# Attention, soft mixture of experts and a cosine-gated layer on one core: another written-out order of the attention's steps, with 86 instead of 91 of the exponentials' sums on VectorE

## The chip, the core and the metric

One core of a Trainium2 chip runs the whole program. The metric is the device time of one execution in microseconds (us), the median over repeated runs. The engines work side by side and meet through semaphores: TensorE (PE, with its weight loads shown as PEld), VectorE (DVE), ScalarE (ACT), GpSimd (POOL) and SyncE (SP), which issues most of the transfers (DMAs). Each engine takes its own instructions strictly in the order in which the program holds them, so an instruction that waits holds up all that stand behind it on that engine.

## What is computed

Three layers, cut to what matters here:

```
q_pool = q.reshape(B, H, S // 2, 2, D).mean(axis=3)          # B=4, H=8, S=1152, D=64
scores = matmul(q_pool, k.transpose) / sqrt(D)
attn   = exp(scores - max);  attn /= sum(attn) + 1e-9
x      = matmul(attn, v)                                     # to (2304, 512)
x      = soft_moe(x, phi, w1, w2)                            # 8 experts of 4 slots, F = 1024
h      = x @ w_in;  out = (h * cos(h)) @ w_out               # d_ff = 2048
```

The change touches the attention alone (with the first part of the mixture of experts and the preparation of later weights, which are woven into it).

## The kernel before, in words

The 32 heads are taken as 16 pairs (p = 0 to 15). Both heads of a pair stand side by side in the 128 partitions. A pair's 576 pooled queries are taken in two halves (a = 0, 1) of 288, and the 1152 keys in nine blocks (t = 0 to 8). What is done for a pair, with the names of the functions that record it and the lines of the profile:

- `load_q`, `load_k`, `load_v`: SP loads 576 KB each. `sum_q` (DVE, L347), `tr_q` and `tr_k` (PE transposes, L358, L382), `q_hi`, `k_hi` (ACT) and `q_lo`, `k_lo` (DVE, L369, L401) make the split operands.
- `max_pair` (PE, L415) makes scores of 128 queries with 384 keys for both heads, and `max_pair_red` (DVE, L424) reduces them to a maximum; 15 such for a pair. `max_neg` (DVE, L430), `max_row` (PE, L442) and `max_put` (ACT, L449) turn the negated maxima into a row that is added to the scores by a matmul.
- `scores` (PE, L460 and L463, eight matmuls), `exps` (ACT, L471), `av` (PE, L498, four instructions in the trace) and `av_out` for each half: the first run of five blocks goes out on ACT (L511), the second run of four is added on DVE (L513).
- `e_sum` (L486 for t = 1, L488 after it; L482 for one of the last pair) adds the exponentials of the nine blocks into a tile ES, one after the other: eight sums a half, each of which reads what the last one wrote. They run on DVE or on POOL; the table `VEC` says which.
- The denominators: `sum4` (PE, L523) sums ES over the partitions, `sum4_copy` (ACT, L530) copies it, `sum4_turn` (L535, a small transfer that ACT issues) spreads it over the partitions as `rt`, `sum4_rec` (DVE, L563) takes the reciprocal, `sum4_hi` (ACT, L567) and `sum4_lo` (POOL, L571) split it, `sum4_back` (L576, two small transfers) brings it back, `sum4_spread` (PE, L584) spreads it, and `pair_mul` (DVE, L589) multiplies the pair's result.
- Woven between: 32 weight conversions (`conv_load`, `conv_act` L289, `conv_low` L294 on ACT; `conv_clamp` L298, `conv_shift` L304, `conv_sign` L310 on DVE; `conv_round` L316 on POOL; `conv_store`), loads of the experts' weights (`ring_piece`, `late_piece`, L251), and for three of the four batches the statistics of the mixture (`b_...`).
- At the end: `run_min`, `run_turn`, `run_row`, `run_col`, `run_put` (L743 to L761) carry a running minimum over, and `fin_sum0`, `rec_mul` (L545 to L596), `l_xt`, `lt_mm`, `lt_max`, `lt_exp`, `l_x` finish the last pair's first half.

Nothing of this order comes from a scheduler at run time. All 2500 steps are made as a list, and `ORDER`, a string of two characters a step, says in which order they are recorded; each engine then gets its share in that order. Two things follow the order too: the four double banks of PSUM ("2") and the five tiles of exponentials ("E") are handed out by it, so the order also decides whose reader a step on TensorE has to wait for.

```
    for i in order:
        o = ops[i]
        assert all(d.done for d in o.deps)
        if o.take:
            o.spot = spots[o.take].pop(0)
        o.fn(o)
...
    def on_vector(p, a, t):
        return (p, a, t) == (NP - 1, 1, 1) or str(t) in VEC[2 * p + a]
```

After the attention (from some 489 us on) come the rest of the last pair, the experts (L1229, L1262) and the cosine layer (L1397 to L1443), whose code is not touched.

Of the kernel before, what the change touches and what calls it, by code (L numbers as in the profile page):

```python
# [52 lines left out]
)  # L53
ORDER = (
    "020304050709060G080H0A0OXsXt0PXu0Q0R0M0N0E0F0C0D0S0I0J0K0L2429010T2A0U0X0Y0V0b0W0m23250B2C0n0p0t0x0qXvXwXxXyXz26"
    "0u0-0y0c100h0i0o0s0w2D0Z0a0d2E0r0+12132F0e27X+2814150v0z2B1118191C1D160f0g1G1H2W0j2XX-Y1Y21A17Y01B1F1J0k0l2M1K2N"
    "2G1L1O1M1P1S1W1a2H1E1I2I1T2UY31X1Q1U474A1N1R1V1Z1b2V1d1e2J2O2PY41f1g2S2T1j1k1n1o2Q2R1Y1r1s2K1i2L1c482Y4D4E4H4I1h"
    "1l2b2c4JY64G1m1q4BY5Y74C2Z2a1u1v1p4F6C2j2k2q2r2t2u2l2m2x2y2-2h306B2i1t1wY81x334WY94K1y4X002s2w2+32YAYB4L3436372v"
    "2z2f2g2d383C393G3KYC2e2n3D31353H1z4f3A4S3B3E3L2obs6E2p3F3J1+YE1-YD4g3N3P3O4T4OYF3Q3S3W3a3I4P3T3XYHYI3b4Q4RYJ3e3U"
    "3Y4Y4Z4a3R3V3Z3dYG8Z3f3hYK203i3c4bYM4U4V3j3k3n3o3M4M3r3s3v4N4c6F3w3g6G6J4d3m3l3q3uYL3yYNYPYO4h49YQ4e3p3t3z4i4u4v"  # L60
    "4j4k4x4-534y4z503x544l4m57213+58226H6L3-YRYUbt514n4w4+6I6K6M6N52565A5B40YSYT4o55595C4p5D5G5K4q5O4r5H6O6a5L5P8c5E"
    "8a5F4s4tAd5J5N5R6b6UYVYW6P5I5M5SYX6V5T5W5U5XYY5a5b5e6S5YYZ5i5f416W6c6T6X5VYa6d5Z425d5hYb5j5lYc43446Y5m5c5g5kbu5n"
    "5r6Z5o5p5s6Q6R5v5Q5w6e6f5z5+6g6D6lbv6m8f8g8iYdYf8d6h6i8eYe5q5u5t5x5y60616y5-8q8h6z8r6-737071776pYgYhYi747B787C6q"
    "45468b6263648j8kAg6jYk8l6+72767A7E7F6k756n6o7G8m7H7K7L7O8n7S7P797D7T6r6s6tYjYl7J6u7N7R6v7V6wbwChbx7I6x8oAe8+7M65"
    "7W7Q667X7a8p7Y7e7i7b8-YnYoYp7m907f7c7j67997Z7d687g7n7k7oYs919AYm7h7l7p7q8w8x7r7sby8y8z7v7z7w817+8s8t8uYqYr7u8v7y"
    "8082AhAi9293947t7x7-83Al84857U9798YtYv9K9L9N9O9PAf696AYu9R9VYw9S9W9B9C9Z9aYxY+8687Aj88An95969M9QAk9TAmAo9UAp9Y9c"
    "9d9X9F9G9e9f9D9E9HYy9i9m9j9b9n898A9q9rCkA+A-8B8CYzAsAt9h9l9I9JY-Z09p9t9g9k9o9vZ1Z29u9w9yAu9zA09sA4A1bzAvA5A8Z3Z6"
    "A9B2B3AwAx9x9-9+8D8EZ4Ayb+AzZ5b-A3A7ABAC8J8KB0B18NA28OA6AAADAEAHAIAqArElALAPAMAQ8P8QB4B5B68FClAFZ78GAJAN8IB7CmCp"
    "Z9ZAB8AGAKAOASZ88H8T8LAT8UBBZBZCBO8MBCCiBPBJBKBRBSBVZDBZBWBaBDBE8VAR8WAUAV8RZE8SB9BABdBeBHAWBTBic0c1BICnBFBXBGCo"
    "ZFZGCqZHZIZJBQBUBLBYBcBjBbBfBgBhCrBmBqBuZKCsCtBkBnZMBrCuC+CvBlc2C-BpBtBvZLBxByBMD6AXBoBsBwEoCyBNAYAZD78X8YBzCzB+"  # L70
    "C0C4C1D4C5D5C8C2C9CCCHCDC6CAD0CwCxEmZNB-C3C7CID1CBCFCGD8ZOD9CLCMD2CPCQCTD3EpDADBCECJCNHAAaZPZQCKCOCSZRZSDCCUCjCR"
    "CVEqEtCWCXDSc3DTc4DDDVDEHDDWDXDZDaDdDFZTDeDhAbCYDGDiErZUAcDHCZCaDbDfc5DjEnEvDUDIDYDcEwExDgDJEsZVEuDKDmDnDLDMc6Dk"
    "Dlc7DNZWDOCbZXDoDqDrDPDuJEDyDvDzCcZYCdZZZaE+E-F4F5CeDpDsDtDxD-DQDRE0F0F1F2E1E2E4F3E5DwD+E6E8ECE9EDEyEzZcEGEHELF6"
# [1455 lines left out]
```

## Time and profile before

| | us |
|---|---|
| median of 3 runs (773.06 to 776.13) | 773.59 |
| the profiled execution, its own time | 778.18 |
| span of the profile (first to last instruction) | 776.4 |
| TensorE busy, of the span | 737.1 (95%) |
| VectorE busy | 587.7 (76%) |
| ScalarE busy | 448.9 (58%) |
| GpSimd busy | 409.5 (53%) |

The profiled execution took 4.59 us more than the median. All durations below are from it. Its span leaves 1.8 us of its time outside. A row of a group of instructions gives their number, the busy time, the mean duration of one, and the idle time of the engine before them with what ended it. The granted clock of TensorE stands as PEclk: 1.00 is 2.4 GHz, 0.50 is 1.2 GHz.

### The profile page before, as it was taken

The page shows a single profiled execution, that of the slowest core. Times are in us where ns is not written, and L with a number is a line of the kernel's source. Part 1 is how long each engine was busy: PE and PEld are TensorE (multiplying, and loading weights), DVE is VectorE, ACT ScalarE, POOL GpSimd, SP SyncE. Part 2 cuts the span into 40 slices and gives each one's busy share as a digit, 9 for nine tenths or more (in the row PEclk, how much of TensorE's full clock was granted, in tenths as well). Part 3 has the DMA queues.
Part 4 walks back from the last instruction along what each step waited for, and adds up shares of the span by engine and source line. Part 5 has one row for each costly group of instructions (what it writes and reads, how often), then busy time and mean ns, then how long its engine had stood idle before and what let it go on. Part 6 is the DMA issues. An engine that isn't in the chain of part 4 may idle for free.

```text
span 776.4 us, 16372 instructions
## 1 busy us (share of the span) xinstructions
PE 737.1 (95%) x6336; PEld 532.1 (69%) x6336; DVE 587.7 (76%) x935; ACT 448.9 (58%) x838; POOL 409.5 (53%) x340
## 2 busy tenths in 40 slices
...
GB/s 201 111 122 142 116 194 143 100 164 174 198 144 137 199 137 140 185 138 162 52 157 103 140 164 211 190 365 385 302 1 28 27 29 28 10 17 28 29 28 27
DMA packets 86482, 101.48 MB, mean 131 GB/s; under 512 B 48260, under 2 KB 48260, under 8 KB 86404
## 3 DMA queue, kind: packets, MB, share of 16 engines
...
q10 hardware_dynamic: 6020, 0.34, 0.6%
...
## 4 chain that ended last, share of the span: by engine, by line
PE 48%; DVE 9%; ACT 2%; issue 2%; POOL 1%; ACTq 0%; DVEq 0%; POOLq 0%
PE o L1433 16%; PE o L1435 8%; PE mx L498 6%; PE mx L460 4%; DVE nm L424 2%; PE po L1262 2%; PE u L1397 2%; PE h L1229 2%; PE mx L415 2%; DVE ES L488 1%; PE mx L463 1%; PE pm L1341 1%; POOL ES L488 1%; ACT E L471 1%; PE mx L442 0%
## 5 line engine op out<-in xcount | busy, mean ns | idle before, releaser
L488 POOL TENSOR_TENSOR ES<-ES,E 128x576 f32<-128x576 f32 x142 | 208.2, 1467 | 94.5 <-DVE ES L488 66.6
L424 DVE TENSOR_REDUCE nm<-mx 128x2 f32<-128x768 f32 x240 | 221.3, 950 | 26.7 <-PE mx L415 25.8
L471 ACT ACTIVATE E<-mx 128x576 f32<-128x576 f32 x288 | 177.4, 651 | 83.3 <-PE mx L463 62.6
L460 PE MATMUL mx<-Q,kX 64*128 64x288 f32 x1152 | 171.5, 314 | 9.9 <-DVE nm L424 4.7
L498 PE MATMUL mx<-E,vn 128*64 128x288 f32 x1152 | 157.7, 414 | 3.0 <-DVE nm L424 2.2
L1417 POOL TENSOR_TENSOR lo<-g,hi 128x512 fp32r<-128x512 f32 (+1 forms) x73 | 94.3, 1291 | 110.4 <-DVE hi L1415 106.1
L460 PEld LDWEIGHTS mx<-Q,kX 64*128 64x128 f32 x1152 | 111.8, 190 | 30.3 <-DVE nm L424 11.5
L498 PEld LDWEIGHTS mx<-E,vn 128*64 128x64 f32 x1152 | 75.8, 137 | 59.1 <-ACT E L471 8.0
L1433 PE MATMUL o<-w_hi,hi 128*128 128x512 f32 x288 | 113.1, 393 | 0.7 <-DVE hi L1415 0.7
L1435 PE MATMUL o<-w_lo,hi 128*128 128x512 f32 x288 | 113.2, 393 | 0.3 <-DVE w_lo L1321 0.3
L415 PE MATMUL mx<-kX,Q 64*128 64x384 f32 x480 | 87.6, 387 | 5.7 <-DVE nm L424 4.7
L460 PE MATMUL mx<-Q,kY 64*128 64x288 f32 x576 | 87.2, 297 | 0.0
L463 PE MATMUL mx<-NM,one_row 64*128 64x288 f32 x576 | 86.9, 296 | 0.0
L1433 PE MATMUL o<-w_hi,lo 128*128 128x512 f32 x288 | 77.4, 389 | 0.0
L1404 DVE SCALAR_TENSOR_TENSOR r<-t,u 128x512 f32<-128x512 f32 (+1 forms) x73 | 49.4, 679 | 36.4 <-ACT t L1402 35.8
L1402 ACT ACTIVATE t<-u 128x512 f32<-128x512 f32 (+1 forms) x73 | 43.0, 591 | 58.0 <-PE u L1397 57.9
L1413 DVE SCALAR_TENSOR_TENSOR g<-r,u 128x512 f32<-128x512 f32 (+1 forms) x73 | 49.6, 679 | 35.5 <-ACT r L1411 34.8
L316 POOL TENSOR_TENSOR cvt<-cvt 128x512 uint32<-128x512 uint32 x32 | 43.4, 1357 | 61.9 <-DVE cvt L310 28.7
L415 PEld LDWEIGHTS mx<-kX,Q 64*128 64x128 f32 x480 | 44.9, 190 | 28.6 <-DVE nm L424 10.9
L488 DVE TENSOR_TENSOR ES<-ES,E 128x576 f32<-128x576 f32 x81 | 61.5, 759 | 2.8 <-POOL ES L488 0.5
L1433 PEld LDWEIGHTS o<-w_hi,lo 128*128 128x128 f32 x288 | 54.1, 188 | 11.5
L1433 PEld LDWEIGHTS o<-w_hi,hi 128*128 128x128 f32 x288 | 54.2, 188 | 10.8 <-DVE hi L1415 0.9
...
## 6 DMA issues: line engine op xcount, KB each, us to landing
...
```

What stands on the lines that cost most here:

```text
L415: nc.tensor.matmul(out=m[:, h, 0:384], lhsT=Q1[p % 2][hs, AT[i]:AT[i] + 128], rhs=X[p][hs, ks], start=True, stop=True)
L424: nc.vector.tensor_reduce(out=nm3[p][:, i, :, c:c + 1], in_=m[:, :, 0:384], axis=AX.X, op=ALU.max)
L460: nc.tensor.matmul(out=sc[:, h, 0:HF], lhsT=x[hs, ks], rhs=y[hs, qs], start=(n == 0), stop=False)
L463: nc.tensor.matmul(out=sc[:, h, 0:HF], lhsT=one_row[hs, :], rhs=NM[p % 2][hs, qs], start=False, stop=True)
L471: nc.scalar.activation(out=e, in_=sc[:, :, 0:HF], func=AF.Exp, scale=1.0 / 16.0)
L488: eng.tensor_tensor(out=ES[p, a], in0=ES[p, a], in1=E[p, a, t], op=ALU.add)
L498: nc.tensor.matmul(out=av_t[p, a, g][64 * h:64 * h + 64, 0:HF], lhsT=vn[p][:, h, t, :], rhs=E[p, a, t][:, h, :], start=(t == g), stop=(t = ...
L1404: nc.vector.scalar_tensor_tensor(out=r, in0=t, scalar=MAGIC, in1=u, op0=ALU.subtract, op1=ALU.subtract)
L1413: nc.vector.scalar_tensor_tensor(out=g, in0=r, scalar=1.0, in1=u, op0=ALU.subtract, op1=ALU.mult)
L1417: nc.gpsimd.tensor_tensor(out=lo[:, 0:n], in0=g, in1=hi[:, 0:n].bitcast(FP32), op=ALU.subtract)
L1433: nc.tensor.matmul(out=o, lhsT=x, rhs=w_hi[ff], start=(ff == 0 and not part), stop=bool(part and ff == NF - 1))
L1435: nc.tensor.matmul(out=o, lhsT=x, rhs=w_lo[ff], start=False, stop=False)
```

## The change

`ORDER` is another string of the same 2500 steps, and `VEC` names other blocks for VectorE. No function is changed. Of the tables:

```
 VEC = (
-    "468", "1", "45", "2468", "25", "237", "4", "1267",
+    "58", "12", "6", "125", "1267", "1", "25", "1458",
...
-    "234", "17", "238", "137", "67", "123568", "2345678", "1234567",
+    "28", "168", "48", "", "1678", "368", "2345678", "1234567",
 )
 ORDER = (
-    "020304050709060G080H0A0OXsXt0PXu0Q0R0M0N0E0F0C0D0S0I0J0K0L2429010T2A0U0X0Y0V0b0W0m23250B2C0n0p0t0x0qXvXwXxXyXz26"
...
+    "Xs0203040705090A0S0B0T0O0P06240E0Q0I0R010GXt0J0F0K0L0H0C0M0N292D232E2A0D0U0V080W0m0pXuXv2F0nXw0q0r2C0t0u0x0h260y"
...
 )
```

Of the 256 sums 91 were on VectorE and 165 on GpSimd; now 86 are on VectorE and 170 on GpSimd. In the new order fewer steps on VectorE stand right behind the step that wrote what they read. Counted over the whole attention, such neighbours are: `conv_clamp` and `conv_shift` 20 before and 9 now, `conv_shift` and `conv_sign` 22 and 11, two sums on the same ES 25 and 13, `max_pair_red` and its `max_neg` 28 and 24, `b_stat` and `b_lg` 1 and 2.

VectorE around the reciprocal of pair 5 (`sum4_rec`, L563), before: the conversion's three steps and the maximum's negation (L430) are neighbours.

```order
L424 TENSOR_REDUCE nm_2664<-mx 128x2 x3
L563 RECIPROCAL rt<-rt 128x9
L298 TENSOR_SCALAR cvt<-cvt 128x512
L430 TENSOR_REDUCE Z<-nm_2664 128x4
L304 TENSOR_SCALAR cvt<-cvt 128x512
L310 SCALAR_TENSOR_TENSOR cvt<-raw,cvt 128x512
L424 TENSOR_REDUCE nm_3102<-mx 128x2 x2
```

The same place of the change:

```order
L430 TENSOR_REDUCE Z<-nm_2637 128x4
L298 TENSOR_SCALAR cvt<-cvt 128x512
L424 TENSOR_REDUCE nm_3058<-mx 128x2
L304 TENSOR_SCALAR cvt<-cvt 128x512
L488 TENSOR_TENSOR ES<-ES,E 128x576
L310 SCALAR_TENSOR_TENSOR cvt<-raw,cvt 128x512
L513 TENSOR_TENSOR avs<-mx,avs 128x288
L424 TENSOR_REDUCE nm_3058<-mx 128x2
L563 RECIPROCAL rt<-rt 128x9
L424 TENSOR_REDUCE nm_3058<-mx 128x2 x7
```

What moved: between the conversion's steps now stand steps that don't read them, and the reciprocal stands behind the conversion instead of ahead of it. Counted from the step that issues the transfer of `rt` (`sum4_turn`), VectorE has 13 steps ahead of this reciprocal, where it had 6. For other pairs it is the other way round: for pair 2 it has 3 where it had 9, for pair 6 it has 5 where it had 8.

VectorE in the last pair, before: four sums in a row (blocks 5 to 8 of the first half) stand ahead of the running minimum's copy (L761) and of pair 14's product (L589).

```order
L751 TENSOR_REDUCE mr<-mx 1x32
L513 TENSOR_TENSOR avs<-mx,avs 128x288
L488 TENSOR_TENSOR ES<-ES,E 128x576 x4
L761 COPY nM_118<-mx 32x1
L589 TENSOR_TENSOR xT<-avs,mx 128x576
L482 SCALAR_TENSOR_TENSOR ES<-E 128x576
L488 TENSOR_TENSOR ES<-ES,E 128x576 x2
L556 TENSOR_SCALAR rec<-mx 128x96
```

The same place of the change:

```order
L751 TENSOR_REDUCE mr<-mx 1x32
L488 TENSOR_TENSOR ES<-ES,E 128x576 x5
L513 TENSOR_TENSOR avs<-mx,avs 128x288
L589 TENSOR_TENSOR xT<-avs,mx 128x576
L488 TENSOR_TENSOR ES<-ES,E 128x576 x2
L482 SCALAR_TENSOR_TENSOR ES<-E 128x576
L761 COPY nM_118<-mx 32x1
L488 TENSOR_TENSOR ES<-ES,E 128x576 x2
L556 TENSOR_SCALAR rec<-mx 128x96
```

What moved: the product (L589) has come ahead of the last two sums of the first half. The copy (L761) has gone behind them, and so has, on TensorE, the small matmul that it reads (L758), which in the change stands behind the scores of blocks 1 to 4 of the second half instead of ahead of them. TensorE there before:

```order
L498 MATMUL mx<-E,vn 64x288 x8
L758 MATMUL mx<-ones,mr 32x1
L460 MATMUL mx<-Q_1_104,kX 128x288 x2
L460 MATMUL mx<-Q_1_104,kY 128x288 x2
L460 MATMUL mx<-Q_1_106,kX 128x288 x2
L463 MATMUL mx<-NM_108,one_row 128x288 x2
L584 MATMUL mx<-rh,pick 128x288 x2
```

And in the change:

```order
L463 MATMUL mx<-NM_108,one_row 128x288 x2
L758 MATMUL mx<-ones,mr 32x1
L498 MATMUL mx<-E,vn 64x288 x4
L545 MATMUL mx<-ES,ones 64x288 x2
L498 MATMUL mx<-E,vn 64x288 x6
L460 MATMUL mx<-Q_1_104,kX 128x288 x2
```

What moved: the sums over the partitions for the last pair's first half (L545) now follow the first two blocks of its second half, ahead of blocks 5 to 8; the matmul of the running minimum (L758) stands next to them.

## Rows read from the trace of the kernel before

**Rows 1.** Busy us (x instructions) of PE, PEld, DVE, ACT, POOL by stretch, clock, DMA share, GB/s.

```profile
20.00:480.00 460.00, 441.04 (x4750) 316.20 (x4752) 410.86 (x599) 282.79 (x524) 287.41 (x211) 0.99 0.51 145
...
210.40:213.70 3.30, 3.30 (x28) 3.30 (x30) 3.26 (x5) 1.30 (x2) 1.50 (x2) 0.50 0.91 279
473.20:476.50 3.30, 3.30 (x30) 3.02 (x28) 1.62 (x3) 1.07 (x3) 0.00 (x0) 0.50 0.72 253
500.00:520.00 20.00, 19.34 (x164) 6.83 (x158) 4.51 (x25) 4.55 (x12) 3.49 (x8) 1.00 1.00 345
```

**Rows 2.** Chain that ended last, 297 to 489 us: its shares by line.

```profile
by line: PE mx L498 23.7%; PE mx L460 15.8%; DVE nm L424 9.9%; PE mx L415 7.1%; DVE ES L488 5.5%; PE mx L463 4.7%; issue 4.4%; POOL ES L488 2.2%; ACT E L471 2.2%; PE mx L442 1.9%; DVE cvt L304 1.5%; DVE cvt L310 1.4%; DVE avs L513 1.4%; PE 
```

**Rows 3.** Waits of VectorE, 20 to 489 us: us in total, times, longest.

```profile
DVE nm L424 <- PE mx L415: 25.8, 47, 1.6
...
DVE rt L563 <- DMA rt<-rec: 2.6, 1, 2.6
```

**Rows 4.** Waits of TensorE, 20 to 489 us.

```profile
PE mx L460 <- DVE nm L424: 4.7, 8, 1.3
```

**Rows 5.** Groups by line: busy us, mean ns | idle before.

```profile
L488 POOL TENSOR_TENSOR ES<-ES,E 128x576 f32<-128x576 f32 x142 | 208.2, 1467 | 94.5 <-DVE ES L488 66.6
...
L488 DVE TENSOR_TENSOR ES<-ES,E 128x576 f32<-128x576 f32 x81 | 61.5, 759 | 2.8 <-POOL ES L488 0.5
```

**Rows 6.** VectorE by time, 455 to 458 us: start, us, what.

```profile
455.31 0.75 DVE L488 TENSOR_TENSOR ES<-ES,E 128x576 f32<-128x576 f32 x1
455.97 0.45 DVE L513 TENSOR_TENSOR avs<-mx,avs 128x288 f32<-128x288 f32 x1
...
457.00 0.42 DVE L298 TENSOR_SCALAR cvt<-cvt 128x512 f32<-128x512 f32 x1
457.34 0.15 DVE L743 TENSOR_TENSOR mrow<-nmst 128x1 f32<-128x1 f32 x1
```

**Rows 7.** The same from 34 us on.

```profile
34.17 0.42 DVE L298 TENSOR_SCALAR cvt<-cvt 128x512 f32<-128x512 f32 x1
34.62 0.43 DVE L304 TENSOR_SCALAR cvt<-cvt 128x512 uint32<-128x512 uint32 x1
```

**Rows 8.** The chain, 466 to 490 us: start, us, what.

```profile
470.29 0.77 DVE ES L488
...
471.16 0.76 DVE ES L488
```

**Rows 9.** VectorE, 466 to 479 us; in brackets the idle time before.

```profile
468.20 0.46 DVE L513 TENSOR_TENSOR avs<-mx,avs 128x288 f32<-128x288 f32 x1 [1.22 <-PE mx L498]
468.58 3.33 DVE L488 TENSOR_TENSOR ES<-ES,E 128x576 f32<-128x576 f32 x4
...
478.11 0.26 DVE L556 TENSOR_SCALAR rec<-mx 128x96 f32<-128x96 f32 x1 [2.94 <-PE mx L545]
```

**Rows 10.** TensorE, 472 to 475 us.

```profile
472.02 0.40 PE L460 MATMUL mx<-Q,kX 64*128 64x288 f32 x2 [2.26 <-DVE nM L761]
...
472.80 0.29 PE L460 MATMUL mx<-Q,kY 64*128 64x288 f32 x2
472.93 0.30 PE L460 MATMUL mx<-Q,kX 64*128 64x288 f32 x2
...
474.39 0.45 PE L460 MATMUL mx<-Q,kY 64*128 64x288 f32 x2
474.63 0.45 PE L460 MATMUL mx<-Q,kX 64*128 64x288 f32 x2
```

**Rows 11.** VectorE, 206 us.

```profile
206.75 0.21 DVE L563 RECIPROCAL rt<-rt 128x9 f32<-128x9 f32 x1 [2.58 <-DMA rt<-rec]
```

**Rows 12.** TensorE, 209 to 211 us.

```profile
209.42 0.44 PE L415 MATMUL mx<-kX,Q 64*128 64x384 f32 x2 [1.53 <-DVE nm L424]
210.29 0.65 PE L415 MATMUL mx<-kX,Q 64*128 64x384 f32 x2 [0.42 <-DVE nm L424]
```

**Rows 13.** ScalarE's queue, 198 us.

```profile
198.34 0.59 ACTq L535 DMA_DIRECT2D rt<-rec  x1
```

More of the change, by code (lines that the diff above doesn't have):

```diff
@@ L59 @@
[L59 to L63, printed above, removed]
@@ new lines @@
+    "3236372e2l2m38393C311z3D353A2n3G3HYD4O2o2p4P3K6E4f3PYFYH3E3Q3L3BYI1+3F3J4g3N3O4W1-204Y4X3S3T3W3a8Z3e3I4Z3X3U3b3M"
+    "3fYJ3Y4a4b4UYG4V3R3V3Z3d3h3i4MYK4N3j3n3k3o21223r3v6C3c3g3s4p4Q3l4R3pYM3w3t3xbs4c3m3q3uYL3y4q3z4nYN4l4d4e4o4m6F6G"
+    "6J4u4x4-494v4y5350YPYQ4z6H57YR544jYO4w584+5256YS5A51554k6I6K5B594h6L6M4i5C5D5E5G6N4r3+5H3-4s4t6c8c6S6dYU6T405K5L"
+    "5OYTYV5IYXYY5F5P5J5N5R5Tbt6n5M5QYW5S5U5W6o5X5a5e5i8a5bYZ5f6Y5Y5j5c414243445V5Z5g6Z6O6P6U6VYc6Qbu5d5h5l5n5k6D5m6R"
+    "5o6e6f5r5sYa5vYb6l5w6m5z5+6W6X8f8g6abv5q5u6bAd8d5p5t5x6g8i8e8h6h5y6i6061Yd45468j8k8l6y6-73Yf6z5-70Yg7177746j787B"
@@ new lines @@
+    "6k7C62Yh63758q6p6q8m8n6+72Ye8r64Yk767AYiYj7E7F6r797D6sbw7G7H8y7K8z7O7S7L7PYl7I657TYm6t8u6u6vYn7J7N7R7V6w8v6x7W90"
+    "918s7X7a7Y7M8t7b7Q7U7e7ibx667fYoYp7j8+Ae7m7r7v8-7c7nYq67688o8p7Z7gAg7d7h7sYs7l7p7q7w8wYr8x7z927+7k7o818295AhAiYt"
+    "Yu7t7x937u7y94Alby968084859B9C9K9LYv9N9O9R9V7-839S9P9W97989Z9a696A86Yw9T8788YxAjAnAk999AAo8bAp9M9Q9U9Y9cAmAy9dAz"
+    "Yy9e9f9i9m9j9X9b9gbz9Db+899nCh9E9q9rY+8AYz8B9F9h9G8C9H9l9p9I9JCkY-Z09tAf9k9u9vAu9y9wAvZ19o9zA09+A1A+A2A4A8A-A5As"
+    "Z2B2B3Z3b-c0A69x9-A3A7A9ABACZ4AtAwAxZ6ADAE8D8EAHAIZ5ALAMAqAAAFArAPAQB0B18F8GB4B58I8HBDAGAK9sCiB6Z7Z9ClZ8B7B8AOAS"
@@ new lines @@
+    "BEc1ATCmCpBOBRBVBPZABSAJANBWBTARBXBHBIElBZBaBdCn8JBe8KCoZBZEBbBiBBBQBUBYBjBCCrBFc2ZCZDCqCsAUAVBGc3CtBcBg8LBh8MBf"
+    "8PBJ8QBmBKBnBqBrBuAWBkBoBsEoBvD2ZFB9BABlBLBpBtD3BxZGBy8T8UHABMBN8N8O8R8SD4D5BwBzC0B+ZHC4C1C5C8C9CyZIZJCzCCCDAXAY"
+    "D8D98V8W8X8YC+C-D0ZKc4C2D1CjCwC6CAB-C3C7CBCFCxCuAZAaZLCGCvCECHZMCID6D7ZNCJDACLCMCPCTZPZQCQCUEpHDZOCNDBCKCRCOEqEt"
+    "CSDCCWCXDSDVDTc5DWDZZRDaCVDFDGDdDeEmAbAcCYDXCZErDLDMEnZUEsEuEvEwExDUDYDcCaDDDEDhDiDNDgDODHDIZSDmDnDJDbDfDjDkDlDK"
+    "E+DqE-DuDyZTZVDrDPDvZXFAFBZWZYDQDoDsDwZZDpDtDxZaZcDzD-E0c6DRE1E2EyE4EzD+E8E5CbE6F0E9EAF1ECZbF2EDF3HBCcCdEGEHFHE3"
@@ new lines @@
+    "FIE7FCFDF4c7F6F7EBEFEJCeEEEKF8JEEIZdF5ELEMEPETF9EQFEEUZfENZgEXEYZeERFLFMHEHFHIZhZkEVZiFFEOESEWEaEbFPFGFWFQFXCfCg"
+    "FZFRFaFdFSFeFhFiFJFlEZFKFmFNFOFTHGHKHLHMEcFbJHHHHJFYFcFgFkFoZjEdHbZlZnEeZmFpFqFrHcFfFuFyG0ZoFjFnFvFsFzHRc8ZpZqHS"
+    "EfHNHOG1FtFxc9F-ZsG3G4FwFUFVHZHaHXEgEhG5G8G6HYG9F+G2GCGDGGGAGHGKGLGEGIZrZtHVHWZvGPGTHdHeG7GBGFGJGQZwEiGUGNGMGOHT"
+    "HUcAGXGYLIHPHQHCGbHkGRHfZxGcJFGVJIZuJJJMHgHhHlGZZyGSGWGaGeGfHsHxHtcBHyHmHnH+I2GdH-I6I0I3I7HoHpZ+IAIBEjEkGgJKGhGi"
+    "HiHqZzZ-HjHzHrHuI1I5JLJNI9IDIEHvcCLLHwJOa1JPJQa2IFIGIJIKINI4GjI8ICGkGlIOJdIHIRISIWJecDIXcEa3IZJZILIPJhJiIIcFIMIQ"
```

65 lines of the change are left out of this document (25 added, 40 removed), and 8 rows, old and new, of the table VEC.

## Prediction

> **What bounds the kernel now.** I read the busy time by stretch first. From 20 to 480 us, which is nearly all of the attention, TensorE is busy for 441.0 of 460 us and VectorE for 410.9 [rows 1]: both are near their limit, ScalarE (283) and GpSimd (287) are not. TensorE's 19 us of idle time are the most that a better order could win there, beside what it loses at the half clock. Then the waits: VectorE waits for TensorE for 25.8 us in 47 pieces, of which none is longer than 1.6 us [rows 3], and TensorE waits for the maxima in short pieces too, at its largest group for 4.7 us in 8 [rows 4]. The two take turns: a step on TensorE needs a bank of PSUM that VectorE has yet to read, and VectorE needs a score that TensorE has yet to make. The chain that ended last says how the turns are shared. Of its stretch from 297 to 489 us the lines of VectorE that the row still shows make 9.9 + 5.5 + 1.5 + 1.4 + 1.4 = 19.7% [rows 2]; the row is cut off, so I take a quarter.
>
> Two places stand out. At 206.75 us VectorE comes to pair 5's reciprocal after 2.58 us of idle time, because the small transfer `rt` has not landed [rows 11]; ACT issued it at 198.34 [rows 13], 8.41 us earlier. TensorE then idles for 1.53 and 0.42 us [rows 12], and from 210.4 to 213.7 us its granted clock is 0.50, the lower of its two levels, with TensorE busy all the time [rows 1]. At 472.02 us it has idled for 2.26 us behind VectorE's copy of the running minimum, for which four sums of 3.33 us had to end first [rows 9, 10], and from 473.2 to 476.5 the clock is 0.50 again. What the lower clock costs stands in the same rows: two pairs of matmuls start 0.13 us apart before (472.80, 472.93) and 0.24 after (474.39, 474.63) [rows 10], so 3.3 us of it give 1.8 us of work and lose 1.5.
>
> **The change part by part.** The profiled execution took 778.18 us, 4.59 more than the median of the runs. I take the sum off both alike.
>
> *Less work on VectorE.* Five sums leave it. One takes 759 ns there and 1467 on GpSimd [rows 5], but where the next step doesn't read it, that one starts 0.66 us later (455.31 to 455.97) [rows 6]; five give 3.3 us. A sum that follows a sum on the same ES starts 0.87 us after it (470.29 to 471.16) [rows 8], 0.21 more. There are 12 fewer of these: 2.5 us. A conversion's second step starts 0.45 us behind its first (34.17 to 34.62) [rows 7], and another step 0.34 behind such a first one (457.00 to 457.34) [rows 6]: 0.11 for a neighbour. The conversions have 22 fewer neighbours and the maxima 4, the statistics one more; at 0.11 for all, 25 give 2.8 us. Together 8.6 us of VectorE's 411. Not all of it reaches the end: at a quarter, 2.2. The bounds are 0 (it all goes into VectorE's own waits for TensorE, 25.8 us) and 8.6 (VectorE decides everywhere).
>
> The Trainium skill ("VectorE: DVE Perf Modes", section "The DRAIN you can't avoid") speaks against the middle of this: each VectorE instruction is followed by a flush before the next may start, whether or not the next one reads it, and a semaphore between them "costs nothing extra here". By that the 5.3 us for neighbours are nothing and this term is a quarter of 3.3, or 0.8: the forecast would be 768.6. The rows differ, 0.87 against 0.66, so I stay with them.
>
> *Five sums more on GpSimd*: 5 x 1.47 = 7.3 us, at no cost, because GpSimd idles for 460 - 287 = 173 us [rows 1]. Its longest piece is the half of pair 13 with all eight sums, 8 x 1.47 = 11.7 us, while a half lasts 460 / 32 = 14.4. If that cover were gone, it would cost at most the 0.7 us by which a GpSimd sum is longer, for each of five, 3.5.
>
> *The last pair.* Between 468.20 and 478.11 us VectorE idles for 1.22 and 2.94 us [rows 9], the second time because the matmul that it needs (L545) stood on TensorE behind the scores that waited and then ran at the lower clock. In the change the product (L589) comes ahead of the last two sums, so the scores no longer wait for four sums. The copy of the minimum comes late, but by then TensorE's four blocks of scores are ahead of it, and only small matmuls, `av` and L545 stand behind. The same sums remain to be done. The bounds are a gain of 1.22 + 2.94 = 4.2 us and a loss of 1 (five sums now stand in a row ahead of L513). I take 2.5, nearer to the gain, since the wait of 2.94 has lost its cause.
>
> *Pair 5's reciprocal.* With 13 steps of VectorE behind the issue of `rt` instead of 6, it lands in time; gone are 1.53 + 0.42 us of idle time and 1.5 for the clock, 3.4 us. Against it stand the pairs whose reciprocal has come closer: 3 steps for pair 2, 5 for pair 6. A wait there is priced like pair 5's. I charge half of one, 1.7, between 0 and two of them, 6.9.
>
> *Around it.* The loads of q, k and v and of the conversions move on SP too. The waits above are for maxima, scores and `rt`, not for these loads, so I cost this at nothing; a `sum_q` or `av` that came ahead of its load would cost like pair 5's reciprocal. The start is the same nine maxima one behind the other. After the attention the experts' stage has the DMA engines at a share of 1.00 with TensorE at 19.34 of 20 us [rows 1]; pieces of weights that go out later would cost time there. In both orders the last ones go out around pair 14's product, so nothing is charged.
>
> The sum: 2.2 + 2.5 + 3.4 - 1.7 = 6.4 us, 773.6 - 6.4 = **767.2**; in the profile 771.8.
>
> **The rivals.** *The turns decide* (no change): VectorE's relief ends in its own waits, the wait at a reciprocal turns up at another pair in full, and only the last pair gains: 773.6 - 2.5 = 771.1. For it speaks that the waits of both engines are short and many [rows 3], so that an order that cures some will make others; against it that the places of 1.5 us and more are few and known. A stage of experts that is held by its transfers would give back the last pair's 2.5 and end at the same side, 773.6.
>
> *VectorE decides everywhere*: 8.6 + 2.5 + 3.4 = 14.5 us, 759.1. For it speaks that VectorE is at 89% of the stretch; against it the 25.8 us in which it waits for TensorE.
>
> *The denominators' transfer is late* (slower): `rt` goes through the same 16 DMA engines as loads of up to 576 KB. A reciprocal that VectorE reaches too early holds up every maximum behind it, as at pair 5, for 3.4 us each time. Its candidates are pairs 2 and 6, and others with five or six steps (10, 11, 14). The gains of 2.2 + 2.5 + 3.4 = 8.1 are used up at the third such place; with four of them it is 773.6 + 13.8 - 8.1 = 779.3. For it speaks the row of 8.41 us, against it that this is the only wait of its kind in 15 pairs [rows 3]. The skill's page "DMA: Bandwidth & Descriptors", section "Queues, rings and completion order", lets each DMA engine alternate between the queues, packet by packet; by that a small transfer would not queue behind another queue's loads and this rival would be worth nothing, but pair 5's took 8.41 us.
>
> **How the numbers follow.** Chances: the sum as worked out 0.49 (763 to 769.6 alone), the turns decide 0.26, VectorE everywhere 0.12, late transfers 0.13. A measurement of this kernel can tell about 0.5% from no change, 3.9 us: faster is below 769.7, slower above 777.5. The first and third case are faster, less a little of the first's upper edge: 0.60; the second is the same, 0.27; the fourth is slower, 0.13. The range reaches down to the third case's time, 759, and up to 777.5, where the fourth begins; that leaves out the fourth and half of the third.
>
> **What would show it.** Neighbouring sums on VectorE still 0.87 us apart, but fewer, and its busy time to the end of the attention less by some 5 us; no idle time over 1 us ahead of pair 5's L563, none or little at the others'; no stretch at the lower clock near 210 us, nor one around the last pair's first scores; the wait ahead of L556 well under 2.94 us; the experts' first matmul (L1229) some 6 us earlier. It is wrong if a wait of 2 us or more stands ahead of L563 at two pairs or more, if `sum_q` or `av` wait for their loads, or if the experts' stage is longer by what the attention has won.

## The result, and the profile of the change

The change takes 748.33 us (median of 4 runs, 746.98 to 750.2) where the kernel before took 774.5 beside it: 0.9663 of the time, 95% interval 0.963 to 0.9697. That is 26 us, four times the 6.4 forecast and below the range. The profiled execution took 750.2 us, with a span of 748.4. The two profiled executions lie 28.0 us apart (778.18 before), 2 us more than the medians, so the profiles show a little more than the gain.

First the busy time by stretch again, before (to the end of the last pair's scores and `av`, 488.7 us) and after (460.0 us); columns as in [rows 1]. Before:

```profile
20.00:488.70 468.70, 447.31 (x4792) 319.87 (x4792) 418.17 (x615) 285.63 (x531) 287.41 (x211) 0.99 0.52 147
100.00:200.00 100.00, 96.80 (x1086) 69.40 (x1084) 91.60 (x128) 64.84 (x121) 70.36 (x52) 1.00 0.56 155
300.00:400.00 100.00, 96.92 (x1066) 69.92 (x1062) 90.00 (x134) 63.86 (x119) 63.06 (x47) 1.00 0.50 143
```

After, with the stretch behind the attention and one of the experts':

```profile
20.00:460.00 440.00, 435.48 (x4790) 315.10 (x4789) 407.30 (x611) 282.62 (x531) 289.64 (x216) 1.00 0.56 158
100.00:200.00 100.00, 99.57 (x1129) 72.32 (x1127) 92.57 (x138) 66.40 (x127) 70.43 (x52) 1.00 0.55 155
300.00:400.00 100.00, 99.66 (x1117) 71.74 (x1115) 92.40 (x140) 65.21 (x125) 71.71 (x55) 1.00 0.55 151
460.00:463.40 3.40, 3.35 (x15) 1.47 (x15) 0.00 (x0) 0.25 (x1) 0.00 (x0) 0.50 0.00 0
490.00:510.00 20.00, 19.82 (x168) 6.44 (x160) 5.16 (x25) 7.86 (x25) 4.69 (x14) 1.00 1.04 383
```

The attention ends 28.7 us earlier, and the stretches in its middle show where: TensorE idles for 0.4 of 100 us where it idled for 3. Over the whole stretch its idle time falls from 468.70 - 447.31 = 21.4 to 440.00 - 435.48 = 4.5 us, and its busy time by 11.8 for the same matmuls. Of this busy time two stretches at 0.50 [rows 1], 1.5 us each, are gone; the new kernel has one left, just behind the attention (460.00), where the kernel before has one too (490.30). I read most of the rest as waits too short to show as idle time, in which a matmul's end stands later instead: in [rows 10] the first pair behind a wait takes 0.40 us, the pairs behind it 0.29 and 0.30. No run shows this by itself. It is seen at the line of TensorE that waits most, by group, before:

```profile
L460 PE MATMUL mx<-Q,kX 64*128 64x288 f32 x1152 | 171.5, 314 | 9.9 <-DVE nm L424 4.7 <-DVE nM L761 2.3 <-DVE avs L513 1.0
```

and after:

```profile
L460 PE MATMUL mx<-Q,kX 64*128 64x288 f32 x1152 | 166.2, 305 | 0.6 <-DVE nm L424 0.3
```

The same 1152 matmuls are busy for 5.3 us less, some of it by the clock. VectorE's busy time falls by 10.9 us and its idle time by 50.5 - 32.7 = 17.8. Its waits (us in total, times, longest) answer to [rows 3], where one group of before is missing that matters now, the wait at L513:

```profile
DVE avs L513 <- PE mx L498: 6.9, 13, 1.3
```

VectorE's waits after:

```profile
DVE nm L424 <- PE mx L415: 16.0, 42, 1.1
...
DVE avs L513 <- PE mx L498: 0.5, 3, 0.2
```

TensorE's waits after, against [rows 4]:

```profile
PE mx L545 <- DVE xn L860: 1.7, 1, 1.7
PE mx L584 <- DMA rh<-hl: 1.2, 1, 1.2
...
PE mx L460 <- DVE nm L424: 0.3, 2, 0.2
```

The 4.7 us behind maxima are 0.3. The chain that ended last, from 270 to 460 us, against [rows 2]: of VectorE only 1.5% for the maxima still appear among the large shares; by this chain TensorE bounds the attention alone.

```profile
by line: PE mx L498 31.8%; PE mx L460 25.5%; PE mx L415 10.5%; PE mx L463 7.9%; DMA rh<-hl 3.3%; PE mx L442 2.3%; PE mx L523 2.0%; PE mx L382 1.8%; PE mx L358 1.7%; DVE nm L424 1.5%; PE mx L584 1.1%; PE mx L836 1.1%; PE mx L677 1.1%; issue 
```

The two places of the prediction. Pair 5's reciprocal (L563) on VectorE, without idle time ahead of it, against [rows 11]:

```profile
197.53 0.45 DVE L513 TENSOR_TENSOR avs<-mx,avs 128x288 f32<-128x288 f32 x1
198.38 0.96 DVE L424 TENSOR_REDUCE nm<-mx 128x2 f32<-128x768 f32 x1 [0.40 <-PE mx L415]
199.25 0.20 DVE L563 RECIPROCAL rt<-rt 128x9 f32<-128x9 f32 x1
199.61 2.69 DVE L424 TENSOR_REDUCE nm<-mx 128x2 f32<-128x768 f32 x3 [0.16 <-PE mx L415]
```

The last pair on TensorE and on VectorE, against [rows 9, 10]: the waits of 2.26 and 2.94 us are gone, but the spread of pair 14 (L584) now comes before its transfer `rh` has landed, and the product (L589) behind it waits too.

```profile
444.44 0.37 PE L584 MATMUL mx<-rh,pick 64*128 64x288 f32 x1 [1.25 <-DMA rh<-hl]
```

VectorE there:

```profile
443.31 0.46 DVE L513 TENSOR_TENSOR avs<-mx,avs 128x288 f32<-128x288 f32 x1 [0.23 <-PE mx L498]
444.98 0.76 DVE L589 TENSOR_TENSOR xT<-avs,mx 128x576 f32<-128x576 f32 x1 [1.21 <-PE mx L584]
```

### The profile page after: what moved, and what is told of

The parts are those of the page before. It is cut to its first block, busy times and chain, and to the rows that moved or that the text cites. A ratio compares the mean times of both kernels' runs of the same rounds, so it can differ in the third digit from the quotient of the medians.

```text
span 748.4 us, 16381 instructions
## 1 busy us (share of the span) xinstructions
PE 724.4 (97%) x6336; PEld 527.1 (70%) x6336; DVE 577.2 (77%) x930; ACT 445.5 (60%) x838; POOL 410.8 (55%) x345
## 4 chain that ended last, share of the span: by engine, by line
PE 86%; DVE 8%; DMA 2%; ACT 2%; issue 1%; ACTq 0%; SPq 0%; DVEq 0%
PE mx L498 18%; PE o L1433 16%; PE mx L460 15%; PE o L1435 8%; PE mx L415 7%; PE mx L463 5%; DVE nm L424 3%; PE po L1262 2%; PE u L1397 2%; PE h L1229 2%; PE mx L442 1%; PE mx L382 1%; PE mx L523 1%; DMA kn<-in_k_dram 1%; PE pm L1341 1%
## 5 line engine op out<-in xcount | busy, mean ns | idle before, releaser
L488 POOL TENSOR_TENSOR ES<-ES,E 128x576 f32<-128x576 f32 x150 | 218.6, 1458 | 58.5 <-DVE ES L488 33.5
L424 DVE TENSOR_REDUCE nm<-mx 128x2 f32<-128x768 f32 x240 | 221.6, 951 | 17.5 <-PE mx L415 16.2
L471 ACT ACTIVATE E<-mx 128x576 f32<-128x576 f32 x288 | 175.5, 652 | 72.6 <-PE mx L463 53.4
L460 PE MATMUL mx<-Q,kX 64*128 64x288 f32 x1152 | 166.2, 305 | 0.6 <-DVE nm L424 0.3
L415 PE MATMUL mx<-kX,Q 64*128 64x384 f32 x480 | 84.4, 380 | 2.0 <-DVE nm L424 1.3
L316 POOL TENSOR_TENSOR cvt<-cvt 128x512 uint32<-128x512 uint32 x32 | 41.5, 1296 | 44.9 <-ACT cvt L294 12.4
L415 PEld LDWEIGHTS mx<-kX,Q 64*128 64x128 f32 x480 | 43.8, 188 | 27.1 <-issue 11.4
L1435 PEld LDWEIGHTS o<-w_lo,hi 128*128 128x128 f32 x288 | 54.2, 188 | 11.2 <-DVE w_lo L1321 1.5
```

Source lines behind the costliest of these rows:

```text
L415: nc.tensor.matmul(out=m[:, h, 0:384], lhsT=Q1[p % 2][hs, AT[i]:AT[i] + 128], rhs=X[p][hs, ks], start=True, stop=True)
L424: nc.vector.tensor_reduce(out=nm3[p][:, i, :, c:c + 1], in_=m[:, :, 0:384], axis=AX.X, op=ALU.max)
L460: nc.tensor.matmul(out=sc[:, h, 0:HF], lhsT=x[hs, ks], rhs=y[hs, qs], start=(n == 0), stop=False)
L471: nc.scalar.activation(out=e, in_=sc[:, :, 0:HF], func=AF.Exp, scale=1.0 / 16.0)
L488: eng.tensor_tensor(out=ES[p, a], in0=ES[p, a], in1=E[p, a, t], op=ALU.add)
L1435: nc.tensor.matmul(out=o, lhsT=x, rhs=w_lo[ff], start=False, stop=False)
```

## The experiments

Eighteen kernels, each timed against the kernel before on the same chip. Ratios are to those runs.

| run | what it is | us | ratio (95%) |
|---|---|---|---|
| b_vec | before's order, the change's `VEC` | 833.9 | 1.0768 (1.072 to 1.0816) |
| b_five6 | before, 5/6 of the columns in VectorE's sums | 771.15 | 0.9948 (0.9928 to 0.9968) |
| b_half | before, half of them | 764.62 | 0.9866 (0.9835 to 0.9897) |
| a_half | the change, half of them | 747.8 | 0.9645 (0.9611 to 0.968) |
| a_load | the change, 86 copies more on VectorE | 751.9 | 0.9705 (0.967 to 0.974) |
| b_apart | before, 43 neighbours parted | 775.69 | 1.0 (0.9975 to 1.0024) |
| b_repair | before, 17 waiting steps moved | 768.39 | 0.9904 (0.9875 to 0.9933) |
| b_av_act | before, L513 on ScalarE | 759.06 | 0.9788 (0.9754 to 0.9822) |
| b_two | before, the two places | 774.09 | 0.9977 (0.9961 to 0.9993) |
| b_two_apart | the two places, neighbours parted | 773.58 | 0.9973 (0.9952 to 0.9994) |
| b_two_avlate | the two places, L513 one step later | 765.81 | 0.9874 (0.9844 to 0.9904) |
| b_all | that, and 42 neighbours parted | 771.04 | 0.9933 (0.9908 to 0.9958) |
| b_two_avact | the two places, L513 on ScalarE | 757.39 | 0.9775 (0.9747 to 0.9803) |
| h_mid | first half before's order, then the change's | 757.88 | 0.9776 (0.9749 to 0.9803) |
| a_av_early | the change, L513 one step earlier | 766.57 | 0.9883 (0.9849 to 0.9917) |
| a_max_late | the change, 25 maxima one step later | 770.04 | 0.9934 (0.9912 to 0.9956) |
| a_max_early | the change, 34 maxima one step earlier | 768.4 | 0.9911 (0.9893 to 0.9929) |
| a_best | the change, two last idle places mended | 745.61 | 0.9623 (0.959 to 0.9656) |

**How much of VectorE's work is worth its time.** Theory A was that VectorE's amount of work decides, theory B that the order does: which step stands next when the other engine is late. The narrower sums, with `n` = 240 (b_five6) or 144 (b_half and a_half):

```diff
-            eng.tensor_tensor(out=ES[p, a], in0=ES[p, a], in1=E[p, a, t], op=ALU.add)
+            n = 240 if eng is nc.vector else HF
+            eng.tensor_tensor(out=ES[p, a][:, :, 0:n], in0=ES[p, a][:, :, 0:n], in1=E[p, a, t][:, :, 0:n], op=ALU.add)
```

> The kernel before, in which the sums of blocks 2 to 8 on VectorE add 480 of the 576 columns and leave the last 96 out. By the two rows for 576 columns (0.76 us) and 288 columns (0.45 us) each is shorter by 0.10 us, 81 of them 8.3 us: about the 8.6 us by which the change was to relieve VectorE, at unchanged places. Theory A: 765 to 767 us, the saving in nearly full. Theory B: VectorE only waits longer for TensorE, a quarter or less comes through, 771.5 to 774 us.

> The kernel before, in which the same sums add 288 of the 576 columns and leave half out: 0.31 us less each, 25 us less on VectorE in the attention. Theory A: some 750 us, as fast as the change, though the order is that of before. Theory B: 766 to 772 us, and VectorE's waits for maxima grow by most of the 25 us.

Measured: 3.6 and 10.1 us less (of 8.3 and 25), so some 40% comes through in the order of before; both times lie just under theory B's ranges, by 0.4 and 1.4 us. The rest goes into VectorE's waits, but not mainly into those for maxima, as the second text had it. With half of the columns these are 32.7 us in 68 pieces where there were 25.8 in 47, and those at L513 (L514 in that kernel) 12.0 in 18 where there were 6.9 in 13:

```profile
DVE nm L424 <- PE mx L415: 32.7, 68, 1.3
DVE avs L514 <- PE mx L499: 12.0, 18, 1.8
```

In the order of the change:

> The changed kernel, in which VectorE's sums of blocks 2 to 8 add half of the columns, 22 us less work on VectorE. If TensorE alone bounds the new order: 746 to 749 us, no gain. If VectorE's work still decides: 740 us or less.

```diff
     def e_sum(p, a, t):
         eng = nc.vector if on_vector(p, a, t) else nc.gpsimd
+        if eng is nc.vector:
+            nc.vector.tensor_copy(out=slT.rearrange("p k s -> p (k s)"), in_=ones)
```

> The changed kernel with a copy of 128 columns that nobody reads added ahead of each of the 86 sums on VectorE, 0.1 to 0.2 us each, 9 to 17 us more work for VectorE. It takes back at least the 8.6 us of relief. Theory A: slower by nearly all of it, 757 to 765 us. Theory B: TensorE is the only bound of the new order and VectorE has some 33 us of idle time in it, so at most 4 us are lost, 748 to 752 us.

Half of the sums' columns less: no gain (747.8). 86 copies more, which were larger than expected:

```profile
L480 DVE COPY slT<-ones 128x128 f32<-128x128 f32 x86 | 22.4, 260 | 0.0
```

The 22.4 us lie partly over the ends and starts of the neighbouring steps: to the last scores of the attention VectorE is busy for 411.9 us where the change has 401.0, so the copies add 10.9 us. They cost 3.6 us of time, and the intervals of the two kernels overlap. The narrower sums take 18.8 us off (382.2) and win nothing. So theory A is out as the cause of the 26 us: neither 25 us less in the old order nor 19 less or 11 more in the new one bridges it.

The narrower sums show one thing more. VectorE waits for maxima for longer with them, and at L513 for 4.7 us in 12 pieces, but TensorE waits behind maxima for 0.7 us in all. Where VectorE waits because it is early, and what stands behind still comes in time, the wait costs nothing. VectorE's waits with the narrower sums in the new order:

```profile
DVE nm L424 <- PE mx L415: 26.5, 61, 1.8
```

**The sums' table alone.**

```diff
 VEC = (
-    "468", "1", "45", "2468", "25", "237", "4", "1267",
+    "58", "12", "6", "125", "1267", "1", "25", "1458",
...
```

> The order of before with the table VEC of the change: the same steps at the same places, but 86 sums on VectorE instead of 91, and other ones. Theory A (VectorE's work decides: what is taken off it comes back at the end nearly in full, wherever it is taken): 5 sums at 0.66 us less, some 771 us. Theory B (the order decides: which step stands next on an engine when the other engine is late): the table is made for another order, so nothing is won, 773 to 778 us. If most of the gain of the change came from the choice of the sums alone, it would show here as 750.

It is 59 us slower: both texts were far too low. The order and the table are one thing. VectorE comes to a sum whose forerunner GpSimd has not done, and everything behind it waits:

```profile
L488 DVE TENSOR_TENSOR ES<-ES,E 128x576 f32<-128x576 f32 x72 | 62.5, 868 | 28.6 <-POOL ES L488 22.5 <-POOL ES L486 3.9 <-ACT E L471 0.8
```

28.6 us of idle time ahead of the sums, where [rows 5] has 2.8. The rest of the 59 us was not followed step by step; stretches at the lower clock are a part of it, for TensorE's mean granted clock over this execution is 0.979, where the profile of before has 0.993.

**Neighbours.** Each is parted like this (43 moves in b_apart, here pair 4's conversion):

```diff
 conv_clamp(9)
+av_out(4, 0, 8)
 conv_shift(9)
-av_out(4, 0, 8)
```

> The order of before in which 43 of the 63 neighbours among conversions and sums on VectorE are parted, each by moving one step past one or two others that are ready; all else stays. Priced as in the prediction (0.11 for a conversion's neighbour, 0.21 for a sum's) that is some 6.5 us less on VectorE, more than the change takes off this way. If neighbours are the cause of the gain: 755 us or less. If they count like other work of VectorE in this order (40% of 8.4 and of 25 us came through in the two runs with narrower sums): 771.5 to 772.5 us. If the Trainium skill's rule holds (a dependence costs nothing extra), no change, 774 to 775 us.

No gain. But the trace had a longer wait for `rt` at pair 5, which might have hidden one:

```profile
DVE rt L563 <- DMA rt<-rec: 4.5, 1, 4.5
```

So the two places were taken first, and the parting was put on top of that, and later on top of the mended L513:

```diff
-sum4_rec(5), sum4_hi(5), sum4_lo(5)
 conv_clamp(13) ... conv_sign(13)
+sum4_rec(5), sum4_hi(5), sum4_lo(5)
...
 e_sum(15, 0, 5)
+run_col, run_put
 e_sum(15, 0, 6), e_sum(15, 0, 7), e_sum(15, 0, 8)
-run_col, run_put
```

> The order of before with the two places of the prediction alone: pair 5's reciprocal (with its two split steps) behind the conversion's last step, and the running minimum's matmul and copy ahead of three of the last pair's four sums. The prediction prices them at 3.4 us for the first; of the second the 2.26 us of idle time and 1.5 us for the clock are touched. If these two make most of what the kernel with 17 moved steps won (6.6 us): 768 to 769.5 us. If the other moves made it: 772 us or more.

> The same two places and the 43 parted neighbours together, since the kernel with parted neighbours alone had a longer wait for rt at pair 5 (4.5 us by its trace, a second stretch at the lower clock), which may hide a gain. If parted neighbours count like other work of VectorE: 2.6 us faster than the kernel with the two places alone. If they are worth nothing: the same time. If they are the cause: 755 us or less.

> The order of before with the two places, the 14 moves of L513 and 42 parted neighbours on top. If neighbours cost once VectorE no longer waits at L513: 2.6 us or more under the 765.8 us of the kernel without the parting. If they cost nothing at the end: 764.5 to 767 us.

The kernel with the two places is 1.2 us faster (0.5 to 3.0 by the interval). Its trace shows that only pair 5's place is mended in it: VectorE doesn't wait there any more. In the last pair the copy of the minimum now comes early, but TensorE's wait goes over to pair 14's product (L589), which still stands behind the sums, and the wait ahead of L556 (2.8 us) and a stretch at the lower clock stay. TensorE's waits for the product, the longest of which, 1.8 us, is this one:

```profile
PE mx L460 <- DVE xT L589: 2.3, 2, 1.8
```

The parting is worth 0.5 us on top, which is within the intervals. On top of the mended L513 it costs some 5, and in that trace pair 5's reciprocal waits for `rt` again, for 2.8 us. Parting steps in this way is no part of the gain: it doesn't even relieve VectorE, which is busy to the last scores for 413.0 us with it and for 412.8 without. But it is no clean test of neighbours. The moves also displace 20 maxima, and TensorE's two largest groups of waits for maxima grow from 7.4 to 10.5 us. What fewer neighbours are worth where no maximum moves is not shown.

**The place of L513.** The kernel with 17 moved steps won 6.6 us, although the two places alone are worth 1.2; nine of the other moves were additions of the second run of `av`.

> The order of before in which 17 steps of VectorE that waited for TensorE (or for rt) by 0.3 us or more are moved behind a step that was ready then (pair 5's reciprocal behind the whole conversion), and the copy of the running minimum stands ahead of three of the four sums. The waits that it takes away are 12 us of VectorE's, with 4.2 us of TensorE's idle time at 209 and 472 us and two stretches at the lower clock (3 us). If single misplaced steps are the cause: 760 to 766 us. If the two places of the prediction alone count: 768 to 770 us. If the order is tight throughout, so that a moved step makes the next one late: 771 us or more.

Its 768.4 us lie where the text had the two places alone, but by the run with these two they are not the reason.

```diff
-            nc.vector.tensor_tensor(out=avs[p][:, a], in0=m, in1=avs[p][:, a], op=ALU.add)
+            nc.scalar.activation(out=avs[p][:, a], in_=m, func=AF.Copy)
```

> The kernel before, in which ScalarE copies the second run of av out (a copy over the first run, the addition is left out), so that VectorE loses the 32 instructions of L513, 14.5 us, at unchanged places. Theory B1 (the order of before was fit for a second run that VectorE does not do, and L513 is what upsets it): 750 to 756 us, nearly the whole gain of the change. Theory B2 (it is work like any other): 40% of 14.5 us come through, 768 to 770 us.

759.1 us, between the ranges of both theories: 16 us (13.8 to 19.1 by the interval) for 14.5 us of VectorE's work, about its whole length, where a sum's time is worth 40%. So it is not its work alone. What it does in the order of before is seen in pair 11, first VectorE:

```profile
351.37 0.89 DVE L424 TENSOR_REDUCE nm<-mx 128x2 f32<-128x768 f32 x1
353.55 0.46 DVE L513 TENSOR_TENSOR avs<-mx,avs 128x288 f32<-128x288 f32 x1 [1.29 <-PE mx L498]
353.93 2.68 DVE L424 TENSOR_REDUCE nm<-mx 128x2 f32<-128x768 f32 x3
```

TensorE before, at the same time:

```profile
350.89 0.52 PE L415 MATMUL mx<-kX,Q 64*128 64x384 f32 x4
351.34 2.16 PE L498 MATMUL mx<-E,vn 128*64 128x288 f32 x16
...
354.25 0.34 PE L415 MATMUL mx<-kX,Q 64*128 64x384 f32 x2
354.93 0.40 PE L460 MATMUL mx<-Q,kX 64*128 64x288 f32 x2 [0.34 <-DVE nm L424]
```

VectorE is free at 352.26 and waits 1.29 us for the last `av`; the scores for the first of the three maxima behind it (353.93) have been there since 351.41 (L415), and TensorE, which needs their bank, idles for 0.34 us ahead of 354.93. In the change the same addition finds its matmuls done:

```profile
336.19 0.46 DVE L513 TENSOR_TENSOR avs<-mx,avs 128x288 f32<-128x288 f32 x1
336.56 0.95 DVE L424 TENSOR_REDUCE nm<-mx 128x2 f32<-128x768 f32 x1
```

Moving L513 alone, with VectorE's work unchanged, one step later in the old order (14 places) and one step earlier in the new one (28):

```diff
-av_out(11, 0, 8)
 max_pair_red(12, 1, 1)
+av_out(11, 0, 8)
```

> The two places, and in 14 of the 16 places where the addition of the second run of av (L513) stood on VectorE before its matmuls were done, it is moved behind one ready step. VectorE's work is unchanged. Its 7 us of waits for av go. If the place of L513 is what made its removal worth 16 us: 8 us or more faster than the kernel with the two places alone, 760 us or less. If only the work of L513 counts: the same time within 2 us.

> The changed kernel, in which 28 of the 32 additions of the second run (L513) stand one step earlier on VectorE, so that, by the trace of the change, they come ahead of their matmuls by 18.6 us in sum, as half of them do in the kernel before. If L513's place is the cause: 758 us or more, and TensorE waits again. If VectorE's slack of 33 us in the new order swallows it: 751 us or less.

8.3 us won and 18 lost, both as the theory of the place had it; the 760 us of the first text took the two places for more than they gave. To the last scores VectorE is busy for 412.4 us with the late additions and for 412.8 without, so there only places changed; with the early ones it is busy for 5.0 us more (406.0 against 401.0). With the early additions VectorE waits 16.6 us there and TensorE waits for maxima again. VectorE's group of waits:

```profile
DVE avs L513 <- PE mx L498: 16.6, 24, 1.0
```

TensorE's:

```profile
PE mx L460 <- DVE nm L424: 3.3, 6, 0.8
PE mx L415 <- DVE nm L424: 1.9, 5, 0.6
```

**Is L513 all?**

> The order of before with the two places and with ScalarE copying the second run of av out (the addition left out), so that VectorE has no L513. The kernel without L513 alone took 759.1 us, and its trace has 1.9 us of TensorE's idle time and a stretch at the lower clock at 201 us and 0.62 at 454 us, which the two places would take away: 755 us if nothing else is wrong with the order of before. If it comes to 750 us or less, L513 and the two places are the whole difference between the two orders; if it stays at 759, the two places are worth nothing in any surroundings.

757.4: even without L513 the order of before stays 9 us behind. Its trace has a wait of 2.3 us for `rt` at pair 5 again, with a stretch at the lower clock (202.4), so a part of the 9 us is that place.

> The first 1211 steps in the order of before (to the start of pair 8's maxima), and all others in the order of the change, with the table VEC of the one or the other for each sum. If the gain is made of many places spread over the attention: about half of 26 us, 759 to 764 us. If it comes from the start or from one place in the first half that is carried on: 768 us or more; if all of it lies in the second half: 752 us or less.

757.9, just under the first text's range: the second half of the order brings about two thirds of the gain. TensorE idles for 7.9 us in the first 220 and for 1.3 in the next 217, so each part of the order brings its own share, and no wait of the first half is carried over:

```profile
20.00:240.00 220.00, 212.10 (x2279) 151.91 (x2279) 201.22 (x282) 136.23 (x251) 149.88 (x108) 1.00 0.55 152
240.00:457.00 217.00, 215.72 (x2406) 156.03 (x2407) 200.86 (x304) 141.45 (x268) 142.69 (x107) 1.00 0.50 144
```

And displaced maxima cost time as well. The two last runs move maxima in the changed order:

```diff
-max_pair_red(1, 0, 1)
 conv_clamp(1)
+max_pair_red(1, 0, 1)
```

> The changed kernel, in which 25 maxima (L424) stand one step later on VectorE, behind a sum or a step of a conversion that was ready: by the trace of the change they start 16.2 us later in sum, VectorE's work is the same and it waits for nothing more. If the time hangs on when a bank of PSUM is read: 754 us or more. If VectorE's slack in the new order swallows a delay as it did the added copies (22 us of work for 3.6): 751 us or less.

> The changed kernel, in which 34 maxima stand one step earlier, ahead of a sum or a step of a conversion, before their matmuls are done: by the trace of the change VectorE would wait 19.2 us in sum, about what the 28 early additions (18.6 us, 18 us slower) made it wait. If a wait of VectorE costs by its length wherever it stands: 763 us or more. If it is L513 that is special, because what was pushed behind it was a maximum whose bank TensorE needed: 754 us or less.

21.7 and 20.1 us slower: 25 steps that are 16.2 us late in sum, and 34 that are 19.2 us early, both counted in the trace of the change, each give back most of the change. Late maxima make TensorE wait for banks; early ones make VectorE wait for scores (25.1 us where it was 16.0), and what is pushed behind them comes late. TensorE's waits with the late maxima:

```profile
PE mx L415 <- DVE nm L424: 7.3, 10, 1.2
PE mx L460 <- DVE nm L424: 5.3, 8, 1.3
```

VectorE's with the early ones:

```profile
DVE nm L424 <- PE mx L415: 25.1, 52, 1.4
```

The second text's rival, that L513 is special, is not borne out, though its bound (754 us or more) holds for this time too: early maxima cost 20.1 us for 19.2 us of waits, early additions 18.2 for 18.6.

Two things limit what these two runs show. VectorE's work is not the same, as the first text had it. The clamps, shifts and signs of the conversions take 72.3 us with the late maxima and 65.7 with the early ones, where the change has 57.7 (the last section shows how that comes about), and to the last scores VectorE is busy for 416.6 and 412.1 us instead of 401.0. At the price of the copies, 3.6 us for 10.9, I estimate some 5 and 4 us of the losses to be that work. The clamps with the late maxima, which take 508 ns in the change:

```profile
L298 DVE TENSOR_SCALAR cvt<-cvt 128x512 f32<-128x512 f32 x32 | 23.2, 726 | 1.7 <-ACT cvt L289 1.3 <-ACT E L471 0.3
```

And it is not the length of VectorE's waits that costs: with the narrower sums in the same order it waits as long for scores, 26.5 us, and loses nothing. What costs is what comes late behind a wait.

**What is left in the change.** Pair 14's spread and product two blocks of scores later, and in the last pair

```diff
-            x0 = add(l_x, c, nc.vector if c else nc.scalar, deps=[m, x0, s4[p - 1]]).uses(m)
+            x0 = add(l_x, c, nc.vector if c == 1 else nc.scalar, deps=[m, x0, s4[p - 1]]).uses(m)
```

> The changed kernel with the two idle places of TensorE that its trace still shows mended: pair 14's spread and product stand two blocks of scores later (1.25 us of idle time behind the transfer of rh), and ScalarE, idle there, makes the last of the three copies of x (L860) that TensorE waits for with 1.69 us and a stretch at the lower clock. At best 1.25 + 1.1 + 1.5 = 3.9 us, 744.5 us; 746.5 us if only one of them comes through; 748 us if what follows waits for something else.

745.6 us, 2.7 less than the change's median, between the two better cases. No stretch at 0.50 is left around the attention's end, where the change has 1.69 us of idle time and 3.4 us at the lower clock:

```profile
458.00:470.00 12.00, 11.29 (x92) 5.88 (x88) 5.64 (x19) 4.76 (x13) 0.00 (x0) 1.00 0.66 205
```

Of all kernels here it is the fastest by its median, though its interval overlaps with that of the change.

## Why the prediction was wrong, step by step

**The bound.** "TensorE's 19 us of idle time are the most that a better order could win there, beside what it loses at the half clock" held for the idle time, of which 16.9 us went, but 11.8 us of busy time went too. The half clock makes 3.0 of these; the other 8.8 I read as waits inside busy time, for which the sum had no place.

**The step that failed** is the first term, "Less work on VectorE", with its bounds of 0 and 8.6. It took the rest of the order as given, VectorE's waits of 25.8 us as a place into which relief disappears, and asked only how much work leaves VectorE. The runs show that the waits are made by the order and go away with it. 25 us less work in the old order win 10 us and 19 us less in the new one nothing, while 14 additions moved by a place, with VectorE's work unchanged, win 8.3. That a step of VectorE should stand where its inputs are ready and where TensorE needs the bank next is shown for L513, 8 of the 26 us, and in the new order for the maxima; for the rest it is inferred. The diff showed this only as "another string". That L513 stood ahead of its matmuls was in the trace of before (6.9 us in 13 waits, the second largest group), and the prediction didn't read it: it took the two largest waits, of 2.6 and 2.9 us, for the two that count.

**The sizes inside that term.** VectorE's work fell by 10.9 us, where 8.6 were foreseen. Five sums are 3.8 of it (priced at 3.3), and 4.7 lie in the conversions (last section). The quarter that was to come through is 40% of a sum's time in the old order; in the new one it is nothing of the sums' and a third of the copies', which is not clear of the intervals. The 5.3 us for neighbours are not borne out: the runs give 0.5 us or a loss, with the limits told above. The Trainium skill's sentence ("VectorE: DVE Perf Modes", "The DRAIN you can't avoid"), by which a semaphore between two steps costs nothing extra, came nearer to that part, though not to the time. The rows of 0.87 and 0.66 us stand; the same section says that a next step which is not held starts earlier, and the trace agrees: the step at 455.97 starts 0.09 us before the sum ahead of it ends [rows 6].

**The last pair**: 2.5 us foreseen. The two waits there (1.22 and 2.94) became 0.23 and none, with 1.21 new ones for `rh`: 2.7. These are waits of VectorE; what they are worth at the end was not tried alone. The prediction took the copy of the minimum for what held TensorE there. With the copy early, the product held it for 1.80 us instead of 2.26: both stood behind the sums, and the change brings the product forward.

**Pair 5's reciprocal**: it has no wait now, and no stretch at the lower clock follows, as foreseen. But mended alone, with only the copy of the minimum moved beside it, it is worth 1.2 us (0.5 to 3.0), not 3.4: the wait and the stretch at the lower clock are gone from that kernel's trace at this place, and less than half of what they were priced at comes through by the median.

**New reciprocals' waits**: none of the 15 waits, so the 1.7 us were charged for nothing; the late transfer is `rh`, at pair 14. The signs of waits and clock that the prediction named came as foreseen, and none of the three that were to show it wrong; they could not tell its sum from this result.

**GpSimd and the experts**: no cost, as foreseen. GpSimd's idle time ahead of its sums fell from 94.5 us [rows 5] to 58.5, with eight more of them in that line's row; and the experts' stage came out 28 us earlier, with the DMA engines at a share of 1.04. GpSimd's group of sums:

```profile
L488 POOL TENSOR_TENSOR ES<-ES,E 128x576 f32<-128x576 f32 x150 | 218.6, 1458 | 58.5 <-DVE ES L488 33.5 <-ACT E L471 5.5 <-DVE rt L563 3.6
```

**The rivals.** "The turns decide" was right in its reason and wrong in its sign: an order that cures some waits makes others, if it is mended by hand (b_two, b_apart, b_all), but the change's order cures nearly all of TensorE's. "VectorE decides everywhere" fell with b_half and a_half.

**Open.** Of the 26 us, 8 are shown for L513's place and about one for pair 5's. The other 17 lie in the order as a whole, spread over both halves (h_mid); the last pair's product is among them, for no run moves it alone. That misplaced maxima cost time is shown in the new order, with VectorE's longer conversions beside it; which steps of the old one make up the 17 was not tried one by one. Nor is it shown what the change's order would lose without fewer sums on VectorE, since the table can't be exchanged alone.
